# Softmax reciprocals as exp(-ln) on the activation engine, and one more pairwise add, in a fused attention and GeGLU block

## The chip, the cores and the metric

The kernel runs on one core of one Trainium2 chip. Its time is the device time of one launch in microseconds (us). The engines are named as in the profile: PE is TensorE (matmuls), PEld its weight loads, DVE is VectorE, ACT is ScalarE, POOL is GpSimd, and SP issues nearly all transfers.

## The reference

The input is 2048 tokens of width 512 in bf16. They are normalised once, and two branches read the result: a sliding, dilated local attention with 32 heads of width 16, where each token looks at itself and at the seven tokens 2, 4, ... 14 places back, and a gated feed-forward layer of hidden width 1376. The output is the input plus both branches.

```python
off = jnp.arange(8) * 2
idx = jnp.arange(S)[:, None] - off[None, :]
logits = jnp.einsum("bhsd,bhswd->bhsw", q, kg) * Dh ** -0.5
logits = jnp.where(idx >= 0, logits, -1e9)
attn = softmax(logits)                       # over the 8 places
o = jnp.einsum("bhsw,bhswd->bhsd", attn, vg)
...
h = gelu(g) * u                              # tanh form
return x + o @ wo + h @ w_down
```

## The kernel before, in words

The tokens are worked off in four blocks of 512 (b = 0 to 3 in all names). The weights stay in SBUF. Of a block, these steps matter here:

- Layer norm of 128-token tiles. For later tiles the sums and the scaling run on ACT (`bnst`, `bnag`, `sub`, `norm` and the small `ve`, `vp`, `va`, `vb`). A DMA transpose (`trx`) then puts the tile into `xnT`.
- Query, key and value products on PE (`mm`, L1009); ACT brings each 128x512 result out of PSUM (`evq`, `evk`, `evv`, L1020).
- Logits: DVE multiplies the queries with the eight shifted keys, one 128x4096 product for each of four head parts (`pr0` to `pr3` within a block, L1040), and adds the products in pairs (`pa_0`, `pa_1`, L1053). PE then sums over the head width with a matrix of ones, `er` (L1085), which accumulates the two pair sums into one pair of PSUM banks, 16 matmuls of 128x32 weights. Ahead of these, `er` also forms a part of the up projection (L1078).
- Softmax: DVE takes the maximum (`d1`, L1117) and subtracts it (`d2`, L1122); ACT takes the exponential into the tile EX (`exp`, L1131); DVE adds the eight exponentials in three steps (`d4a`, `d4b`, `d4c`, L1138) into the tile `ms`, takes the reciprocal in fp16 into `rc` (`d5`, L1150), and multiplies (`d6`, L1155) into the tile PB. SP stores PB to a scratch tensor in DRAM (`ss`, L1164) and loads it again, spread over the head width (`sl`, L1176), into the tile PT.
- Values: DVE multiplies by PT (`pv`, L1184) and adds (`pw`, `pz`), into the tile OT.
- Feed-forward: gate and up matmuls on PE (`fg`, `fu`, L1217), brought out of PSUM by ACT, the gate through gelu (`gelu`, L1227 and L1264), the up part by a plain copy (`uev`, L1234 and L1272). DVE multiplies them (`h`).
- Output: PE accumulates the feed-forward and attention parts (`acc`, L1302); ACT copies most results out (`fe`, L1335), DVE adds the input (`fin`), SP stores.

Each engine works off its own queue strictly in order. The orders are written out as five lists of task names, the table `ORDER`. A planner, `Graph.schedule`, takes these lists as they are; it walks them only to give buffers to tasks and to find which semaphore waits are needed. PSUM is one pool of eight banks, and a task that needs a bank waits for the readers of the one it is given. The pools for `ms`, PB and EX hold one buffer each.

Activations carry a label `table` ("sqrt", "exp", "gelu"), which only the planner's own costs use; loads of ACT's function tables are put into the program when it is built.

Of the kernel before, what the change touches and what calls it, by code (L numbers as in the profile page):

```python
# [135 lines left out]
class Graph:  # L136
# [252 lines left out]
    def report(self):  # L389
# [8 lines left out]
ACTF = mybir.ActivationFunctionType  # L398
# [6 lines left out]
    "pe":  # L405
        "warm0 warm1 warm2 warm3 warm4 warm5 warm6 warm7 warm8 warm9 tpx0_0 warm10 warm11 warm12 warm13 "
        "warm14 mma0_0 tpx0_1 mmt0_0 mmt0_1 mmt1_0 tpx1_0 mmt1_1 mmt0_2 tpx1_1 mmt1_2 mmt0_3 mmt1_3 "
        "mm0_2_0_0 mm0_2_3_0 mm0_2_2_0 mm0_2_1_0 fg0_0 fg0_1 fg0_2 fu0_0 fg0_3 fu0_1 fu0_2 fg0_4 fu0_3 fg0_5 "
        "fu0_4 fu0_5 fg0_6 fg0_7 er0_3 mm1_0_0_0 mm1_1_0_0 mm1_0_1_0 mm1_1_1_0 fg1_0 fu0_6 mm1_0_3_0 "
        "mm1_0_2_0 mm1_1_3_0 fu0_7 fu1_0 fg1_1 fg0_8 fu1_1 mm1_1_2_0 fu0_8 mm1_2_0_0 fg1_2 fg0_9 fu1_2 "  # L410
        "mm1_2_2_0 fg1_3 fu1_3 fu0_9 fg0_10 fg1_4 fu1_4 mm1_2_3_0 fg1_5 mm1_2_1_0 fg1_6 fu1_5 fu1_6 fg1_7 "
        "mm2_0_0_0 mm2_1_1_0 mm2_1_0_0 mm2_0_3_0 er1_3 mm2_0_1_0 fg1_10 mm2_1_2_0 mm2_2_1_0 mm2_0_2_0 fu1_7 "
        "fg2_0 accd1 mm2_1_3_0 accd2 fg2_1 mm2_2_3_0 mm2_2_2_0 fg1_8 fg2_2 acca0 fu2_0 accb0 fg1_9 mm2_2_0_0 "
        "accd3 er2_3 fu2_1 fu1_8 fu1_9 fu2_2 fg2_3 fu2_3 mm3_1_2_0 mm3_1_1_0 mm3_1_3_0 mm3_0_1_0 mm3_0_0_0 "
        "fg2_4 mm3_1_0_0 fu2_4 mm3_0_2_0 fg3_0 mm3_0_3_0 fu3_0 fg3_1 fg2_10 fg3_2 accd7 accd5 mm3_2_0_0 "
        "fg2_5 fu3_1 fg3_3 mm3_2_3_0 mm3_2_1_0 fu2_5 fu3_2 acca4 er3_3 accb4 fg3_4 accd6 fu3_3 fu3_4 fg2_6 "
        "fg3_5 fu2_6 fg2_7 fg3_6 fu2_7 fg2_8 fu2_8 fu3_5 fg3_7 fu3_6 mm3_2_2_0 fg2_9 fu3_7 fu2_9 fg3_8 fu3_8 "
        "fg3_9 fg3_10 acca8 accd10 accd9 fu3_9 accb8 accd11 acca12 accd13 accd14_0 accd14_1 accw14_0 "
        "accw14_1 accw13 accb12 accd15_0 accw12 accw15_0 accd15_1 accw15_1 accd15_2 accw15_2",
    "act":  # L420
        "c_tbl sx1 sq0 negm1 sxx1 sq1 evx0_0 evx0_1 evq0_0 sq2 evq0_1 evk0_0 evx1_0 sq3 evk0_1 bnst8 evx1_1 "
        "bnst9 evq0_2 sq6 evk0_2 evq0_3 evk0_3 ve8 evv0_0_0 sq4 vp8 bnag8 bnag9 va8 gelu0_0 evv0_2_0 "
        "evv0_3_0 bnst10 gelu0_1 bnst11 uev0_2 gelu0_3 vb8 gelu0_4 uev0_1 uev0_3 ve10 gelu0_5 uev0_4 uev0_0 "
        "uev0_5 gelu0_2 halo1 vp10 gelu0_7 bnag10 bnag11 evq1_0_0 evk1_0_0 evv0_1_0 evq1_1_0 evk1_1_0 "
        "gelu0_6 exp0 sub11 evq1_3_0 evk1_3_0 evq1_2_0 va10 uev0_7 uev1_0 uev0_10c uev0_6 sub9 vb10 sub8 "
        "uev1_1 evk1_2_0 norm9 uev0_10b gelu1_1 gelu1_0 norm8 gelu0_8 evv1_0_0 gelu1_2 sub10 uev0_8 bnst12 "
        "gelu0_9 norm11 uev1_2 uev0_9 norm10 evv1_2_0 gelu1_4 gelu1_3 uev1_3 evv1_1_0 uev1_4 uev1_5 uev0_10a "
        "bnst13 gelu1_5 gelu0_10 uev1_6 evk2_1_0 evv1_3_0 evk2_0_0 ve12 vp12 gelu1_7 bnag12 evq2_0_0 gelu1_6 "
        "evq2_1_0 uev1_10b bnag13 uev1_10c halv1 evk2_2_0 evq2_2_0 halo2 exp1 bnst14 sub12 bnst15 uev1_7 "
        "va12 ve14 vb12 uev1_10a vp14 bnag14 evk2_3_0 bnag15 evq2_3_0 evv2_1_0 va14 vb14 fe1 fe2 sub14 "  # L430
        "gelu2_0 evv2_2_0 halo3 gelu1_10 sub15 uev2_0 norm12 sub13 evv2_0_0 evv2_3_0 norm13 fe0 norm15 fe3 "
        "norm14 gelu1_8 gelu2_1 gelu1_9 uev2_1 uev1_8 uev2_2 uev1_9 uev2_3 gelu2_2 evk3_2_0 evk3_1_0 "
        "uev2_10b gelu2_3 exp2 evq3_1_0 evk3_3_0 evq3_2_0 evq3_0_0 halv2 evk3_0_0 uev2_10c evq3_3_0 uev2_4 "
        "uev2_10a gelu2_10 gelu3_1 uev3_0 gelu3_0 fe7 evv3_0_0 gelu2_5 gelu3_3 evv3_1_0 uev2_5 uev3_1 fe5 "
        "gelu2_4 gelu3_2 uev3_10c halv3 evv3_3_0 uev3_2 fe4 fe6 uev3_3 uev3_10b exp3 gelu3_5 uev2_6 gelu3_4 "
        "gelu2_7 uev2_7 uev2_8 gelu3_6 gelu2_6 evv3_2_0 gelu3_7 uev3_4 gelu2_8 gelu2_9 uev2_9 uev3_10a "
        "uev3_7 uev3_5 uev3_6 gelu3_10 fe10 gelu3_8 gelu3_9 uev3_9 fe9 uev3_8 fe8 fe11 fe13 fe12",
    "dve":
        "c_wdz bnst0 bnag0 sub0 rstd0 norm0 mean1 sub1 evy0_0 rstd1 norm1 evy0_1 bnst2 bnag2 sub2 rstd2 "
        "norm2 bnst3 bnag3 sub3 rstd3 norm3 bnst7 bnst6 bnst5 bnag6 bnag7 bnst4 bnag5 sub7 rstd6 bnag4 sub6 "  # L440
        "norm7 sub4 sub5 norm6 pr0_2 pr0_0 pr0_3 rstd4 pr0_1 norm4 norm5 pa0_1 pa0_0 h0_0 h0_1 h0_2 mask "
        "d1_0 d2_0 pr1_0 pr1_1 d4a_0 d4b_0 d4c_0 d5_0 rstd8 d6_0 pr1_3 pa1_0 pr1_2 h0_3 pa1_1 pv0_1 rstd10 "
        "pv0_3 h0_4 pv0_0 h1_1 pv0_2 pw0_1 h0_10 pw0_2 d1_1 pw0_3 d2_1 pz0 pr2_2 d4a_1 pr2_0 d4b_1 h1_3 "
        "d4c_1 h1_2 d5_1 h1_0 d6_1 pr2_1 pr2_3 pa2_0 fin1 rstd12 pa2_1 h1_10 pv1_1 rstd14 pv1_3 d1_2 pv1_0 "
        "d2_2 pv1_2 pw1_1 fin3 pw1_2 h2_1 pw1_3 h1_4 d4a_2 pz1 d4b_2 pr3_1 d4c_2 pr3_2 d5_2 fin0 d6_2 pr3_3 "
        "pr3_0 h2_0 h2_10 pa3_0 fin2 pa3_1 pv2_0 pv2_2 d1_3 pv2_1 d2_3 pw2_1 h3_1 d4a_3 h3_0 d4b_3 fin7 "
        "d4c_3 h2_2 d5_3 fin5 d6_3 pv2_3 pw2_2 h2_3 pw2_3 h2_4 pz2 fin4 pv3_3 pv3_0 pv3_1 fin6 pw3_1 fin10 "
        "h3_3 h3_10 pv3_2 h3_2 fin9 h3_4 pw3_2 fin8 pw3_3 fin11 pz3 fin14_0 fin14_1 fin13 fin15_0 fin15_1 "
        "fin12 fin15_2",
    "pool":  # L450
        "c_ones c_onef c_id c_vnpad c_idb c_eps c_mhalf c_e8a c_e8b c_e8c c_e8d c_ktpad c_mask0 c_mask1 "
        "c_utz sq8 sq10 sq12 sq14",
    "sp":
        "ld_x0_0 ld_x0_1 ld_wq ld_x1_0 ld_wk ld_x1_1 ld_wv ld_x2 ld_x4 ld_x3 ld_wg0 ld_wu0 ld_wt0 ld_x5 "
        "ld_wt1 trx3_0 ld_wt2 trx3_1 trx2_0 trx2_1 ld_wd0 ld_x6 ldxr1 ld_x7 ld_wd1 ld_wo ss0_2 ss0_3 ss0_0 "
        "ss0_1 ldxr2 sl0_1 sl0_3 sl0_2 trx4_0 sl0_0 trx4_1 trx5_1 trx5_0 ss1_2 ss1_3 ss1_1 ss1_0 sl1_1 sl1_3 "
        "sl1_0 sl1_2 ldxr3 trx6_0 trx6_1 trx7_1 trx7_0 sto3 sto1 ldxr0 ldxr7 ss2_1 ss2_2 ss2_3 ss2_0 sl2_0 "
        "sl2_3 sl2_2 sto0 sl2_1 sto2 ldxr5 ldxr4 sto5 ss3_0 ss3_1 ss3_2 ss3_3 ldxr10 sl3_3 sl3_0 sl3_2 sl3_1 "
        "ldxr6 sto4 sto6 ldxr8 ldxr9 sto9 ldxr11 ldxr14 sto8 sto7 sto10 ldxr13 sto11 sto14_0 sto14_1 ldxr15 "
        "ldxr12 sto13 sto15_0 sto15_1 sto12 sto15_2",  # L460
}
SCHED = dict(DMA_BPUS=290e3, DMA_FIXED=1.7)

# [5 lines left out]
def d_act(n):  # L469
    return 0.10 + 0.00085 * n  # L470
# [10 lines left out]
def bass_parallel_sum__sliding_local_dilated__glu_gated_geglu__prompt_kernel(nc, A_x, A_wqkv, A_wo, B_x, B_w_gate, B_w_up, B_w_down, out, dbg=None, cfg=None):  # L481
    cfg = dict(cfg or {})
# [26 lines left out]
    PACT = cfg.get("PACT", 4)  # L509
    PPOW = cfg.get("PPOW", 4)  # L510
    FIN2 = cfg.get("FIN2", tuple(range(14)))
    PR_ADD3 = cfg.get("PR_ADD3", ())
    WO_LAST = cfg.get("WO_LAST", (3,))
    CHAIN_SHIFT = cfg.get("CHAIN_SHIFT", [0, 300, 600, 900])
    FFN_BASE = cfg.get("FFN_BASE", 500)
# [8 lines left out]
    with contextlib.ExitStack() as es:  # L524
        block = es.enter_context(nc.Block())

        def sb(name, shape, dt):
# [14 lines left out]
        mask = sb("mask", [32, 2, 4, 16], F32)  # L542
        one_l = nc.const_aps.tensor(1.0, [128, 128], BF)
        one_r = nc.const_aps.tensor(1.0, [128, 512], BF)
        onef = sb("onef", [128, 2], F32)
# [4 lines left out]
        sums = sb("sums", [128, 3], F32)  # L550
# [6 lines left out]
        rc = sb("rc", [128, NMS, 128], FP16)  # L557
# [27 lines left out]
        G = Graph()  # L585
# [30 lines left out]
        I_onef = Item("onef")  # L616
# [25 lines left out]
            out=cf[:, :], in_=cf[:, :], pattern=[[-1, 128]], compare_op=ALU.is_equal, fill=0.0, base=0,  # L642
            channel_multiplier=1), rd=[I_cf], wr=[I_cf], prio=PC)
        G.task("pool", "c_idb", 0.65, lambda e: e.tensor_copy(out=ident[:, :], in_=cf[:, :]),
               rd=[I_cf], wr=[I_ident], prio=PC)
# [4 lines left out]
            out=E8f[:, :], in_=E8f[:, :], pattern=[[-4, 32]], compare_op=ALU.is_ge, fill=0.0, base=0,  # L650
            channel_multiplier=1), rd=[I_E8f], wr=[I_E8f], prio=PC2)
        G.task("pool", "c_e8c", 0.25, lambda e: e.affine_select(
            out=E8f[:, :], in_=E8f[:, :], pattern=[[4, 32]], compare_op=ALU.is_ge, fill=0.0, base=3,
            channel_multiplier=-1), rd=[I_E8f], wr=[I_E8f], prio=PC2)
        G.task("pool", "c_e8d", 0.25, lambda e: e.tensor_copy(out=E8[:, :], in_=E8f[:, :]),
               rd=[I_E8f], wr=[I_E8], prio=PC2)
        G.task("pool", "c_ktpad", 0.15, lambda e: e.memset(KT[:, KTI[0].slot, :, 0:16], 0.0), wr=[(KTI[0], "pad")],
               prio=PC2)
        G.task("pool", "c_vnpad", 0.15, lambda e: e.memset(VN[:, VNI[0].slot, :, 0:16], 0.0), wr=[(VNI[0], "pad")],
               prio=PC2)  # L660
# [4 lines left out]
            out=mask[:, :, :, :], in_=mask[:, :, :, :], pattern=[[8, 2], [2, 4], [1, 16]],  # L665
            compare_op=ALU.is_ge, fill=-1.0e9, base=-14, channel_multiplier=0),
            rd=[I_mask], wr=[I_mask], prio=PC2 + 10)
# [275 lines left out]
        for b in range(NB):  # L943
# [159 lines left out]
            def msv(k, it=it_ms):  # L1103
                return bass.AP(ms, (it.slot * 2 + k) * 128, [[NMS * 2 * 128, 128], [1, 128]])
# [22 lines left out]

            it_ex = Item("ex%d" % b, P_ex, "ex")

            def mk_d3(lgv=lgv):  # L1130
                return lambda e: e.activation(out=EX[:, :], in_=lgv(0, 128, [(1, 1024)]), func=ACTF.Exp)  # L1131
            G.task("act", "exp%d" % b, d_act(1024), mk_d3(), rd=[it_lg], wr=[it_ex], prio=base + 32,
                   table="exp", batch=b)

            for k, w in enumerate((512, 256, 128)):
                def mk_d4(w=w, it=it_pb, msv=msv):
                    def f(e):
# [6 lines left out]
                       rd=[it_ex if w == 512 else I_su], wr=[(it_ms, 1) if w == 128 else I_su],  # L1144
                       prio=base + 33)

            def mk_d5(msv=msv, it=it_ms):
                def f(e):
                    with nc.allow_low_precision(reason="the reference holds the sums of exponentials in bf16"):
                        return e.reciprocal(out=rc[:, it.slot, :], in_=msv(1))  # L1150
                return f
            G.task("dve", "d5_%d" % b, 0.87, mk_d5(), rd=[(it_ms, 1)], wr=[(it_ms, 2)], prio=base + 34)

            def mk_d6(it=it_ms, ito=it_pb):
                return lambda e: e.tensor_tensor(  # L1155
# [261 lines left out]
```

## Time and profile before

| | us |
|---|---|
| median of three runs | 184.02 (183.99 to 184.84) |
| the profiled execution | 184.58 |
| its span | 182.7 |
| PE busy | 178.9 |
| DVE busy | 169.6 |
| ACT busy | 128.4 |
| table loads on ACT, ten | 12.8 |

The span runs from the first to the last recorded instruction; some 1.8 us of the execution lie around it. Busy time is the union of an engine's instructions; ends of matmuls are modelled, so PE's busy time is not time at its peak. The granted clock was 1.00.

### The profile page before, as it was taken

The page shows a single profiled execution, that of the slowest core. Times are in us where ns is not written, and L with a number is a line of the kernel's source. Part 1 is how long each engine was busy: PE and PEld are TensorE (multiplying, and loading weights), DVE is VectorE, ACT ScalarE, POOL GpSimd, SP SyncE. Part 2 cuts the span into 40 slices and gives each one's busy share as a digit, 9 for nine tenths or more (in the row PEclk, how much of TensorE's full clock was granted, in tenths as well). Part 3 has the DMA queues.
Part 4 walks back from the last instruction along what each step waited for, and adds up shares of the span by engine and source line. Part 5 has one row for each costly group of instructions (what it writes and reads, how often), then busy time and mean ns, then how long its engine had stood idle before and what let it go on. Part 6 is the DMA issues. An engine that isn't in the chain of part 4 may idle for free.

```text
span 182.7 us, 2790 instructions
## 1 busy us (share of the span) xinstructions
PE 178.9 (98%) x1068; PEld 90.6 (50%) x1068; DVE 169.6 (93%) x172; ACT 128.4 (70%) x258; POOL 9.5 (5%) x23
## 2 busy tenths in 40 slices
PE   8999999999999999999999999999999999999994
PEld 2886444544444444444444544444444444444664
DVE  3769999999999999999999999999999999999922
ACT  5688987999999899998695977527449764234011
POOL 6000010003300000122000000000000000000000
PEclk9999999999999999999999999999999999999999
DMA  4999905932562000002851020128000346022433
GB/s 125 360 376 381 125 18 118 367 127 49 183 145 57 0 0 4 0 12 76 256 62 30 4 82 0 30 62 285 28 0 0 92 131 213 0 86 61 140 104 100
DMA packets 26221, 19.60 MB, mean 107 GB/s; under 512 B 13825, under 2 KB 23009, under 8 KB 26209
## 3 DMA queue, kind: packets, MB, share of 16 engines
q1 hardware_dynamic: 26208, 19.44, 37.0%
q8 instruction: 8, 0.13, 0.3%
q14 instruction: 5, 0.03, 0.1%
HBM read 14.71 MB, written 3.15 MB: 98 GB/s over the span
## 4 chain that ended last, share of the span: by engine, by line
PE 91%; DMA 4%; SPq 2%; ACT 1%; issue 0%; DVE 0%; DVEq 0%
PE PS L1217 38%; PE PS L1302 28%; PE PS L1009 19%; DMA XIN<-in_A_x_dram 4%; PE PS L1256 2%; PE PS L1085 2%; PE PS L1078 1%; PE PS L959 1%; SPq L731 1%; SPq L687 1%; ACT XS L769 0%; SPq L737 0%; ACT xnT L919 0%; DVE OB L1346 0%; DVEq L376 0%
## 5 line engine op out<-in xcount | busy, mean ns | idle before, releaser
L1302 PE MATMUL PS<-Wd,HT 128*128 128x512 bf16 (+2 forms) x209 | 41.0, 346 | 0.0
L1217 PE MATMUL PS<-xnT,Wg 128*128 128x512 bf16 x160 | 39.8, 379 | 0.0
L1217 PE MATMUL PS<-xnT,Wu 128*128 128x512 bf16 x160 | 39.1, 379 | 0.0
L1009 PE MATMUL PS<-xnT,Wqkv 128*128 128x512 bf16 x160 | 38.0, 380 | 0.0
L1184 DVE TENSOR_TENSOR UNI<-VN,PT 128x4096 f16<-128x4096 bf16 x16 | 36.3, 2287 | 0.0
L1040 DVE TENSOR_TENSOR UNI<-QT,KT 128x4096 f16<-128x4096 bf16 x16 | 36.1, 2286 | 0.0
L1302 PEld LDWEIGHTS PS<-Wd,HT 128*128 128x128 bf16 x209 | 19.6, 98 | 19.2 <-issue 0.4
L1234 ACT ACTIVATE UU<-PS 128x512 bf16<-128x512 f32 x40 | 23.1, 600 | 6.4 <-PE PS L1217 6.1
L1193 DVE TENSOR_TENSOR UNI<-UNI 128x4096 f16<-128x4096 f16 x12 | 27.5, 2290 | 0.0
L1227 ACT ACTIVATE GG<-PS 128x512 bf16<-128x512 f32 x40 | 22.9, 602 | 5.9 <-DVE HT L1241 5.8
L1009 PEld LDWEIGHTS PS<-xnT,Wqkv 128*128 128x128 bf16 x160 | 17.9, 113 | 16.9 <-issue 0.8
L1217 PEld LDWEIGHTS PS<-xnT,Wu 128*128 128x128 bf16 x160 | 15.6, 98 | 19.0 <-ACT XIN L853 0.4
L1217 PEld LDWEIGHTS PS<-xnT,Wg 128*128 128x128 bf16 x160 | 15.7, 98 | 18.7
L1335 ACT ACTIVATE OB<-PS 128x512 bf16<-128x512 f32 x14 | 8.3, 601 | 17.3 <-PE PS L1302 15.1
L1053 DVE TENSOR_TENSOR UNI<-UNI 128x4096 f16<-128x4096 f16 x8 | 18.2, 2286 | 0.0
L1302 PE MATMUL PS<-Wo,OT 128*128 128x512 bf16 (+2 forms) x76 | 16.5, 346 | 0.0
L1020 ACT ACTIVATE VN<-PS 128x512 bf16<-128x512 f32 x16 | 9.3, 597 | 6.5 <-PE PS L1009 6.5
L1241 DVE TENSOR_TENSOR HT<-GG,UU 128x1024 bf16<-128x1024 bf16 x20 | 13.6, 686 | 0.0
L832 POOL TENSOR_TENSOR sq<-ve,mhalf 128x2 bf16<-128x2 f32 x4 | 6.6, 1657 | 72.8 <-ACT ve L828 72.8
L1302 PEld LDWEIGHTS PS<-Wo,OT 128*128 128x128 bf16 x76 | 7.1, 98 | 6.6 <-issue 0.3
L1272 ACT ACTIVATE UT<-PS 64x256 bf16<-64x256 f32 (+1 forms) x12 | 5.4, 447 | 6.7 <-PE PS L1256 3.9
L959 PE MATMUL PS<-xnT,Wqkv 128*128 128x128 bf16 x128 | 8.3, 222 | 0.3 <-ACT xnT L919 0.2
(85 smaller groups left out, 159.5 us busy)
## 6 DMA issues: line engine op xcount, KB each, us to landing
PT<-pt_scratch SPq DMA_DIRECT2D x16, 256.0 KB, 4.2
XR<-in_A_x_dram SPq DMA_DIRECT2D x16, 128.0 KB, 2.2
out_dram<-OB SPq DMA_DIRECT2D x14, 128.0 KB, 1.9
Wqkv<-in_A_wqkv_dram SPq DMA_DIRECT2D x3, 512.0 KB, 5.0
XIN<-in_A_x_dram SPq DMA_DIRECT2D x6, 256.0 KB, 6.7
Wg<-in_B_w_gate_dram SPq DMA_DIRECT2D x1, 1280.0 KB, 8.6
Wu<-in_B_w_up_dram SPq DMA_DIRECT2D x1, 1280.0 KB, 11.6
Wd<-in_B_w_down_dram SPq DMA_DIRECT2D x1, 1280.0 KB, 6.6
```

What stands on the lines that cost most here:

```text
L959: ins = e.matmul(PS[:, 512 * it.slot + 128 * g:512 * it.slot + 128 * g + 128], lhsT=wcols(which, kt, g), rhs=xnT[:, itx.slot, kt, t * 128: ...
L1009: ins = e.matmul(PS[:, 512 * it.slot:512 * it.slot + 512], lhsT=wcols(which, kt, g), rhs=xnT[:, itx.slot, kt, :], start=(kt == 0), stop=(k ...
L1020: return e.activation(out=o, in_=PS[:, 512 * it.slot:512 * it.slot + 512], func=ACTF.Identity, scale=(QSC, 1.0, 1.0)[which])
L1040: return lambda e: e.tensor_tensor(out=UNI[:, it.slot, :, :], in0=bass.AP(QT, (itq.slot * 4 + g) * 512, [[NQT * 4 * 512, 128], [0, 8], [1, ...
L1053: return lambda e: e.tensor_tensor(out=UNI[:, i0.slot, :, :], in0=UNI[:, i0.slot, :, :], in1=UNI[:, i1.slot, :, :], op=ALU.add)
L1184: return lambda e: e.tensor_tensor(out=bass.AP(UNI, ito.slot * 4096, [[NUNI * 4096, 128], [2048, 2], [512, 4], [1, 512]]), in0=bass.AP(VN, ...
L1193: return lambda e: e.tensor_tensor(out=UNI[:, i0.slot, :, :], in0=UNI[:, i0.slot, :, :], in1=UNI[:, i1.slot, :, :], op=ALU.add)
L1217: ins = e.matmul(PS[0:M, 512 * it.slot:512 * it.slot + 512], lhsT=Wx[:, kt, j * 128:j * 128 + M], rhs=xnT[:, itx.slot, kt, :], start=(kt = ...
L1227: return lambda e: e.activation(out=GG[:, ito.slot, q, :], in_=PS[:, 512 * it.slot:512 * it.slot + 512], func=ACTF.Gelu_apprx_tanh)
L1234: return lambda e: e.activation(out=UU[:, ito.slot, q, :], in_=PS[:, 512 * it.slot:512 * it.slot + 512], func=ACTF.Identity)
L1241: return lambda e: e.tensor_tensor(out=HT[:, ito.slot, j - 1:j + 1, :], in0=GG[:, ig.slot, :, :], in1=UU[:, iu.slot, :, :], op=ALU.mult)
L1302: ins = e.matmul(PS[:, 512 * it.slot:512 * it.slot + CW], lhsT=(OT[:, ito.slot, q, ti * 128:(ti + 1) * 128] if kind == "o" else HT[:, ith. ...
```

## The change

In every block the reciprocal on DVE (`d5`) is replaced by two activations: `ln` takes the logarithm of the sums in place, and `d5`, now on ACT, takes the exponential of minus that into `rc`. A new activation `pre` takes the logarithm of a single constant into an unused place, and `exp` is ordered after it. All of them bear the table label "exp".

In the fourth block (b = 3) a third pairwise add on DVE, `pa3_2`, adds the two pair sums together, so that `er3` needs only one of them: 8 matmuls of L1085 instead of 16. The lists for PE, ACT, DVE and SP are written anew; POOL's list is the same.

```diff
-    PR_ADD3 = cfg.get("PR_ADD3", ())
+    PR_ADD3 = cfg.get("PR_ADD3", (3,))
...
+            t_pre = G.task("act", "pre%d" % b, 0.2, lambda e: e.activation(
+                out=onef[:, 1:2], in_=onef[:, 0:1], func=ACTF.Ln), rd=[(I_onef, 0)], wr=[(I_onef, 1)],
+                prio=base + 32, table="exp")
+
             def mk_d3(lgv=lgv):
                 return lambda e: e.activation(out=EX[:, :], in_=lgv(0, 128, [(1, 1024)]), func=ACTF.Exp)
...
+            G.order_after(t_ex, t_pre)
...
+            def mk_ln(msv=msv):
+                return lambda e: e.activation(out=msv(1), in_=msv(1), func=ACTF.Ln)
+            G.task("act", "ln%d" % b, 0.21, mk_ln(), rd=[(it_ms, 1)], wr=[(it_ms, 1)], prio=base + 34, table="exp")
+
             def mk_d5(msv=msv, it=it_ms):
-                def f(e):
-                    with nc.allow_low_precision(reason="the reference holds the sums of exponentials in bf16"):
-                        return e.reciprocal(out=rc[:, it.slot, :], in_=msv(1))
-                return f
-            G.task("dve", "d5_%d" % b, 0.87, mk_d5(), rd=[(it_ms, 1)], wr=[(it_ms, 2)], prio=base + 34)
+                return lambda e: e.activation(out=rc[:, it.slot, :], in_=msv(1), func=ACTF.Exp, scale=-1.0)
+            G.task("act", "d5_%d" % b, 0.21, mk_d5(), rd=[(it_ms, 1)], wr=[(it_ms, 2)], prio=base + 34, table="exp")
```

The lists around the softmax. ACT, block 0 and block 1:

```diff
-exp0 sub11 evq1_3_0 evk1_3_0 evq1_2_0 va10 uev0_7 uev1_0 ...
+pre0 exp0 sub8 bnag11 evk1_3_0 ln0 va10 uev0_5 evq1_3_0 d5_0 uev0_6 ...
-halo2 exp1 bnst14 sub12 bnst15 uev1_7 va12 ve14 vb12 ...
+bnst15 evv2_0_0 pre1 vb12 exp1 evq2_3_0 ve14 vp14 bnag14 ln1 bnag15 d5_1 va14 fe2 ... uev1_10b pre2 uev2_0 ...
```

ACT, blocks 2 and 3:

```diff
-gelu2_3 exp2 evq3_1_0 evk3_3_0 evq3_2_0 evq3_0_0 halv2 evk3_0_0 ...
+pre3 uev2_4 halo3 evv3_1_0 evq3_2_0 exp2 evk3_2_0 evq3_0_0 evk3_0_0 gelu2_5 evv3_0_0 evq3_1_0 evk3_1_0 uev3_0 ln2 evv3_3_0 d5_2 gelu2_10 ...
-uev3_10b exp3 gelu3_5 uev2_6 ...
+exp3 uev3_3 fe6 ln3 uev2_6 d5_3 gelu2_7 ...
```

DVE, blocks 0 to 3:

```diff
-h0_0 h0_1 h0_2 mask d1_0 d2_0 pr1_0 pr1_1 d4a_0 d4b_0 d4c_0 d5_0 rstd8 d6_0 ...
+h0_1 pr1_0 mask h0_0 d1_0 d2_0 pr1_1 d4a_0 d4b_0 d4c_0 pa1_0 d6_0 ...
-d2_1 pz0 pr2_2 d4a_1 pr2_0 d4b_1 h1_3 d4c_1 h1_2 d5_1 h1_0 d6_1 ...
+d2_1 pr2_2 d4a_1 d4b_1 d4c_1 pr2_1 d6_1 ...
-d4a_2 pz1 d4b_2 pr3_1 d4c_2 pr3_2 d5_2 fin0 d6_2 pr3_3 pr3_0 h2_0 h2_10 pa3_0 fin2 pa3_1 ...
+d4a_2 pr3_2 d4b_2 pz1 d4c_2 pr3_0 h2_1 d6_2 pr3_1 pa3_1 pa3_0 h2_10 fin0 pa3_2 ...
-d2_3 pw2_1 h3_1 d4a_3 h3_0 d4b_3 fin7 d4c_3 h2_2 d5_3 fin5 d6_3 ...
+d2_3 pv2_0 h2_2 d4a_3 pw2_1 d4b_3 fin3 d4c_3 pv2_2 h3_0 d6_3 ...
```

## The prediction

> **What bounds the kernel now.** I read the busy shares first, then the chain that ended last, then busy time by stretch, and last the timelines of ScalarE and VectorE around the softmax of one block.
>
> ```profile
> PE 178.9 (98%) x1068; PEld 90.6 (50%) x1068; DVE 169.6 (93%) x172; ACT 128.4 (70%) x258; POOL 9.5 (5%) x23
> ...
> PE 91%; DMA 4%; SPq 2%; ACT 1%; issue 0%; DVE 0%; DVEq 0%
> ```
>
> TensorE (PE) is the bound: from about 13 us on, the chain is one unbroken row of matmul groups, 0.86 us for four of 128x512. A microsecond that PE waits is a microsecond at the end. The averages hide a second fact, which the busy time by stretch shows (columns: stretch, length, then PE, PE weight load, DVE, ACT and POOL busy):
>
> ```profile
> 36.84:82.61 45.77, 45.77 (x238) 21.84 (x237) 45.52 (x38) 43.85 (x91) 5.22 (x3) 1.00 0.21 56
> 82.61:104.70 22.09, 22.09 (x129) 10.41 (x128) 21.83 (x17) 17.55 (x30) 0.70 (x1) 1.00 0.38 87
> 104.70:140.00 35.30, 35.30 (x190) 16.37 (x189) 35.28 (x29) 21.17 (x38) 0.00 (x0) 1.00 0.20 64
> ```
>
> From 36.84 us (the table load ahead of the first exp) to 82.61 us (the table load ahead of block 2's first gelu), PE and VectorE (DVE) have no slack and ScalarE (ACT) idles only 45.77 - 43.85 = 1.92 us. ACT's 70% is an average over this full stretch and a loose later part (4.5 us idle in the next 22, 14.1 us in the 35 after). Around the first softmax:
>
> ```profile
> 36.84 1.28 ACT L1131 ACT_TABLE_LOAD   x1
> 38.13 1.02 ACT L1131 ACTIVATE EX<-PS 128x1024 f16<-128x1024 f32 x1
> ...
> 40.48 0.95 DVE L1150 RECIPROCAL rc<-ms 128x128 f16<-128x128 f32 x1
> 41.35 0.11 DVE L803 RECIPROCAL rstd<-sq 128x2 f32<-128x2 bf16 x1
> 41.47 0.69 DVE L1155 TENSOR_TENSOR PB<-EX,rc 128x1024 bf16<-128x1024 f16 x1
> ```
>
> A table load takes 1.28 us of ACT, and the next instruction starts at its end. The reciprocal costs DVE 0.87 us (40.48 to 41.35), and the multiply that uses it follows without a wait.
>
> [...] The trace agrees on the load (x4 at exp, 1283 ns each)[...], so I use 1.283 us in all. [...] I read the built program's instruction order: there each Ln and each Exp that follows the other has a load ahead of it[...]. The shared set isn't used. [...] the trace agrees that it is dear: 950 ns for 128 elements, an add of that size 288 ns.
>
> **The change part by part.**
>
> *Table loads on ACT.* Before: 10 loads (one sqrt, four exp, five gelu). After, in the built order: 23. Block 0: Ln for `pre0`, Exp for `exp0`, Ln for `ln0`, Exp for `d5_0`, then gelu: three more than before. Block 1 the same, three more, and `pre2` comes soon after: a fourth. Gelus stand between the rest of blocks 2 and 3, where there are ten loads for four: six more. Together 13 x 1.283 = 16.7 us.
>
> *New activations.* `pre` on one element, four at 0.20 us (row L668, 203 ns) = 0.8 us. `ln` and `d5` on 128 elements are not in the trace[...]. Bounds: 0.2 us (an ACTIVATE of 2 elements) and 0.38 us (of 256).
>
> *Stretch 36.84 to 82.61.* The same content after the change holds 10 loads for 3, that is 7 x 1.283 = 9.0 us, three `pre` 0.6 us, two `ln` and two `d5` 1.2 us: 10.8 us more on an engine with 1.92 us to spare, so ACT is 8.8 us late at its end. The reordered queues don't shift this work out: the rest of that content is nearly the same. ACT empties PE's eight PSUM banks; PE can run ahead by at most eight groups, 8 x 0.865 = 6.9 us, and less in fact, because some banks hold logits and waiting gelus. What banks don't absorb, PE waits for.
>
> *VectorE.* It loses four reciprocals, 4 x 0.87 = 3.5 us, and gains `pa3_2`, which costs 2.20 us (one 128x4096 add start to start): 1.3 us less work. But it gains waits: `d6` needs `d5`, now behind other work and two loads on ACT. Let E be the end of `exp`. Steps are start-to-start times of the rows before.
> - Block 0: ACT runs `sub8` 0.61, `bnag11` 0.78, `evk1_3` 0.49, load and `ln0` 1.57, `va10` and two evictions 1.1, load and `d5_0` 1.57: ready at E + 6.1. DVE has three adds 1.1 and `pa1_0` 2.2: E + 3.3. Wait 2.8.
> - Block 0 again, ahead of E: `exp0` now stands behind two loads and `pre0`. With the Ln load at 36.8 as the Exp load was, E is 36.8 + 1.28 + 0.20 + 1.28 + 1.02 = 40.6. DVE ends `d2_0` near 36.7 (35.06 before, plus 2.2 for `pr1_0`, minus 0.6 for `h0_2`) and `pr1_1` at 38.9. Wait 1.7.
> - Block 1: ACT 1.6 of small work, 1.57, `bnag15` 0.78, 1.57: E + 5.5; DVE 1.1 + 2.2. Wait 2.2.
> - Block 2: ACT three evictions 1.45, gelu load and gelu 1.76, four evictions 1.9, 1.57, 0.48, 1.57: E + 8.7; DVE 6.9 of placed work. Wait 1.8.
> - Block 3: ACT E + 5.7, DVE E + 6.2. No wait; cover is `pv2_2` and `h3_0`, 2.8 us, and if it were gone the wait would be 2.3.
>
> Sum of waits 8.5, minus 1.3 of work: DVE +7.2 us. Its last big step before ends at 173.26 us (`pz3`) and PE's first reader starts at 173.74: nothing there absorbs it. Queued behind the waiting `d6` on DVE are the next block's products, which PE's `er` groups need, and the gated products and sums.
>
> *TensorE.* `er3` drops 8 of its 16 L1085 matmuls (0.86 us for 16): -0.43 us on the path. It waits now for `pa3_2`, at worst 2.2 us later; before, it started 1.4 us after its last sum. That is inside DVE's sum.
>
> *Queues.* SP's issues are reordered, none is added. The stores of `PB` follow `d6` and shift with it; from their issue (42.18) to the first `pv` (51.48) took 9.3 us, and the work now placed after `d6_0` is 8.5 us, after the others 9.5 or more: 0 to 0.8 us of new wait in block 0; I take 0. POOL's queue is the same.
>
> *Sum.* ACT says 8.8 less what banks absorb, DVE says 7.2 less some overlap or more through late evictions. These are two sides of one delay, not addends. I take +7.9, less PE's 0.43: +7.5 us. On the profiled execution (span 182.7, 184.58 in all) that is 192.1; the median, 184.02, lies 0.56 below that execution, so 191.5.
>
> **The rivals.**
> 1. *Banks and cover absorb most (0.13).* Half of the DVE waits vanish because ACT runs closer to its inputs: 4.2 - 1.3 = +2.9: 187. For it: before, PE never waited although ACT was 96% busy. Against it: 8.8 us is more than eight banks.
> 2. *ACT's lag all lands on PE and block 2 adds its own (0.10).* 8.8 + 1.8 for `d6_2` + 2.2 for `pa3_2`: +12.8, near 197[...]. Against it: ACT's 18.7 us of idle between 82.61 and 140.
> 3. *Not slower (0.07).* The lag at the end of block 1 stays under the 6.9 us of banks and DVE keeps its 1.3 us: PE then gains its 0.43 us, 183.6. It decides at one place: `er1` and `er2` must not find their product sums late. A closer packing of the new order could add the 0.4 us of gaps PE has left, and perhaps a shorter start: under 183.1. Against it: 1.92 us of idle for 10.8 us of work.
> 4. *The change doesn't do what it says*: the second half of it (one set for ln and exp) indeed does not hold in the built order. That is my main case.
>
> **How the numbers follow.** Main case 0.70, 191.5, own range 188.5 to 195. About 0.5% (0.9 us) is what a measurement of this kernel can tell from no change, so cases 1, 2 and main are slower: 0.93. Rival 3 gives 0.04 within 0.5% and 0.03 faster. Range: 187 (rival 1's value) to 196.5 (just short of rival 2's).
>
> **What would show it.** In the profile after: 23 table loads, 29.5 us; no L1150 reciprocals; ACT near 148 us busy; DVE idle on ACT ahead of the multiply into PB, some 2 us in each of blocks 0 to 2, none in block 3; PE idle on ACT between 45 and 95 us, 6 to 8 us; L1085 with 56 matmuls; the span near 190. I am wrong if the loads number 12, if loads overlap with activations, or if PE shows no idle in that stretch.

## The result and the profile after

The changed kernel takes 191.92 us (191.82 to 192.19), 1.042 times the kernel before (95% interval 1.0389 to 1.045). Its profiled execution took 192.02 us with a span of 190.3, 7.6 longer than before. The forecast was 191.5, range 187 to 196.5.

Busy time and, below it, the shares of the chain that ended last, from the page of the changed kernel:

```profile
PE 178.0 (94%) x1043; PEld 88.9 (47%) x1060; DVE 169.0 (89%) x169; ACT 146.1 (77%) x283; POOL 9.2 (5%) x23
...
PE 43%; DVE 26%; ACT 20%; DMA 7%; issue 1%; SPq 1%; DVEq 0%
```

PE has lost no work to speak of, but 12 us of its span are idle where it was 4. The chain, which was 91% PE, now passes through ACT and DVE for 46% of the span. The same three stretches as before (PE, PE weight load, DVE, ACT, POOL busy):

```profile
36.84:82.61 45.77, 43.36 (x222) 19.95 (x225) 42.03 (x33) 44.74 (x91) 2.93 (x2) 1.00 0.22 54
82.61:104.70 22.09, 19.87 (x91) 8.91 (x91) 19.31 (x15) 20.62 (x38) 2.15 (x1) 1.00 0.37 81
104.70:140.00 35.30, 34.29 (x200) 16.10 (x203) 33.45 (x28) 28.36 (x47) 0.00 (x0) 1.00 0.20 60
```

PE loses 2.4, 2.2 and 1.0 us in them, DVE 3.7, 2.8 and 1.9. Who waits for whom is in DVE's waits (us in total, times, longest):

```profile
DVE PB L1161 <- ACT rc L1157: 6.4, 3, 2.8
...
DVE HT L1285 <- ACT GG L1270: 1.2, 1, 1.2
...
DVE SU L1143 <- ACT EX L1135: 0.6, 1, 0.6
```

PE's own waits, beside its start, are nearly all for ACT, 6.8 us in all: for banks or results that an eviction, a gelu or `exp` has still to finish.

```profile
PE PS L1223 <- ACT GG L1233: 2.0, 1, 2.0
PE PS L1223 <- ACT UU L1240: 1.9, 2, 1.2
PE PS L1308 <- ACT OB L1341: 1.5, 1, 1.5
PE PS L1009 <- ACT EX L1135: 0.7, 2, 0.5
PE PS L1009 <- ACT GG L1233: 0.7, 1, 0.7
```

On DVE the multiply into PB (`d6`, now L1161) waits three times for the new exponential. ACT's timeline in block 0 shows what stands ahead of it, DVE's what that does:

```profile
36.80 1.28 ACT L1135 ACT_TABLE_LOAD   x1
38.09 1.02 ACT L1135 ACTIVATE EX<-PS 128x1024 f16<-128x1024 f32 x1
...
40.93 1.28 ACT L1153 ACT_TABLE_LOAD   x1
42.23 0.31 ACT L1153 ACTIVATE ms<-ms 128x128 f32<-128x128 f32 x1
...
43.62 1.28 ACT L1157 ACT_TABLE_LOAD   x1
44.91 0.31 ACT L1157 ACTIVATE rc<-ms 128x128 f16<-128x128 f32 x1
...
40.15 2.28 DVE L1053 TENSOR_TENSOR UNI<-UNI 128x4096 f16<-128x4096 f16 x1
45.25 0.69 DVE L1161 TENSOR_TENSOR PB<-EX,rc 128x1024 bf16<-128x1024 f16 x1 [2.83 <-ACT rc L1157]
```

Between `exp` and `d5` ACT switches its table twice, for two activations of 0.31 us. DVE has one add as cover (`pa1_0`, done at 42.4) and then stands still for 2.83 us, with the next products behind it in its queue.

### The profile page after: what moved, and what is told of

The parts are those of the page before. It is cut to its first block, busy times and chain, and to the rows that moved or that the text cites. A ratio compares the mean times of both kernels' runs of the same rounds, so it can differ in the third digit from the quotient of the medians.

```text
span 190.3 us, 2774 instructions
## 1 busy us (share of the span) xinstructions
PE 178.0 (94%) x1043; PEld 88.9 (47%) x1060; DVE 169.0 (89%) x169; ACT 146.1 (77%) x283; POOL 9.2 (5%) x23
## 4 chain that ended last, share of the span: by engine, by line
PE 43%; DVE 26%; ACT 20%; DMA 7%; issue 1%; SPq 1%; DVEq 0%
PE PS L1223 19%; PE PS L1308 14%; PE PS L1009 8%; DVE UNI L1190 7%; DVE UNI L1199 5%; DVE UNI L1040 5%; DMA Wg<-in_B_w_gate_dram 5%; DVE UNI L1053 3%; ACT L1157 3%; DMA Wqkv<-in_A_wqkv_dram 3%; ACT L1130 2%; ACT L1153 1%; ACT L1135 1%; ACT UU L1240 1%; DVE PS L1122 1%
## 5 line engine op out<-in xcount | busy, mean ns | idle before, releaser
L1223 PE MATMUL PS<-xnT,Wg 128*128 128x512 bf16 x158 | 38.4, 379 | 3.5 <-ACT GG L1233 2.0
L1308 PE MATMUL PS<-Wd,HT 128*128 128x512 bf16 (+2 forms) x205 | 40.5, 345 | 0.3
L1009 PE MATMUL PS<-xnT,Wqkv 128*128 128x512 bf16 x156 | 37.2, 380 | 1.8 <-ACT EX L1135 0.7
L1199 DVE TENSOR_TENSOR UNI<-UNI 128x4096 f16<-128x4096 f16 x12 | 27.4, 2280 | 0.0
L1053 DVE TENSOR_TENSOR UNI<-UNI 128x4096 f16<-128x4096 f16 x9 | 20.4, 2283 | 0.0
L1161 DVE TENSOR_TENSOR PB<-EX,rc 128x1024 bf16<-128x1024 f16 x4 | 2.8, 688 | 6.4 <-ACT rc L1157 6.4
```

Of the source, the lines that this page charges most:

```text
L1009: ins = e.matmul(PS[:, 512 * it.slot:512 * it.slot + 512], lhsT=wcols(which, kt, g), rhs=xnT[:, itx.slot, kt, :], start=(kt == 0), stop=(k ...
L1053: return lambda e: e.tensor_tensor(out=UNI[:, i0.slot, :, :], in0=UNI[:, i0.slot, :, :], in1=UNI[:, i1.slot, :, :], op=ALU.add)
L1199: return lambda e: e.tensor_tensor(out=UNI[:, i0.slot, :, :], in0=UNI[:, i0.slot, :, :], in1=UNI[:, i1.slot, :, :], op=ALU.add)
L1223: ins = e.matmul(PS[0:M, 512 * it.slot:512 * it.slot + 512], lhsT=Wx[:, kt, j * 128:j * 128 + M], rhs=xnT[:, itx.slot, kt, :], start=(kt = ...
L1308: ins = e.matmul(PS[:, 512 * it.slot:512 * it.slot + CW], lhsT=(OT[:, ito.slot, q, ti * 128:(ti + 1) * 128] if kind == "o" else HT[:, ith. ...
```

## The experiments

My theory was that the switches of table are the cause: 23 loads where the program needs 12. The rivals were the way over ACT as such (a result that waits behind other work), the newly written orders, and the added add. A second question was how the loads cost: by ACT's total time or by DVE's wait ahead of `d6`. Each ratio is to the kernel before on the same chip, whose median there was 184.3 to 184.4; differences between runs are differences of their medians. A needless load is one of a set that is already there.

**One shared set.** Only the choice of set changes: a load of one set that serves both `ln` and `exp` is put in by hand ahead of `pre0`, `pre1`, `pre3`, `ln2` and `exp3` (in the edit it stands at the first dots). The trace then has 12 loads, these five, six for gelus and one at the start; no other load stands ahead of a `pre`, `exp`, `ln` or `d5`.

```diff
+            def shared(name, f):
+                def g(e):
+                    if name in SHARED:
...
+                    return f(e)
+                return g
...
-"exp%d" % b, d_act(1024), mk_d3(),
+"exp%d" % b, d_act(1024), shared("exp%d" % b, mk_d3()),
...
+SHARED = ('pre0', 'pre1', 'pre3', 'ln2', 'exp3')
```

> Same queues, same activations and the same add as the changed kernel; only the table set is chosen by hand, one that serves both ln and exp, so ACT has 12 loads in place of 23 (11 x 1.283 = 14.1 us less on ACT). If the loads are the cause (my theory): the 7.9 us come back but for at most 1 us, so 183.6 to 185, and DVE's waits for rc shrink from 6.4 us to under 1 us. If the way over ACT is the cause (the result waits behind other ACT work, loads or not): still 188 or more, with over 3 us of waits for rc. If the new orders or the added DVE add are the cause: no change, 191 to 192.

Measured: 183.94 us, ratio 0.9976 (0.9966 to 0.9986). All 7.9 us came back, and the kernel is a little faster than before. DVE's wait for `rc`, and the first stretch, in this kernel:

```profile
DVE PB L1170 <- ACT rc L1166: 0.5, 1, 0.5
```

```profile
36.84:82.61 45.77, 45.77 (x239) 21.67 (x237) 45.63 (x36) 41.94 (x94) 7.41 (x3) 1.00 0.21 59
```

The way over ACT, the new orders and the added add are all still there; none of them costs the 7.9 us. PE is unbroken again, and ACT idles 3.8 us in this stretch, twice what it did before the change.

**The same set, 23 loads again, behind the waits.** `SHARED` now names every `pre`, `exp`, `ln` and `d5`.

> The shared set as in the run before, but with a load of it ahead of every pre, exp, ln and d5, so that the loads number 23 again, at the same places as in the changed kernel; nothing else differs. If a load costs its 1.28 us whatever set it brings: 191.9, within 0.5. If the switch between different sets[...] has a cost of its own: clearly under 191.9, near 184 to 188.

Measured: 196.43 us, ratio 1.0652 (1.0621 to 1.0684), 4.5 us over the changed kernel; I had expected 191.9 or less. The trace shows a difference that I had overlooked: these loads stand behind the semaphore wait of their activation, where those of the changed kernel stand ahead of it (its `ln3` loads at 144.15 us and only then waits 0.58 us, last section). In block 3 of this run:

```profile
141.43 1.28 ACT L1134 ACT_TABLE_LOAD   x1 [1.24 <-DVE PS L1123]
...
147.50 1.28 ACT L1134 ACT_TABLE_LOAD   x1 [1.88 <-DVE ms L1152]
```

ACT waits 1.24 and 1.88 us and only then loads. DVE's waits for `rc` are 8.1 us, four of them, where they were 6.4 and three. Behind these loads PE stands still for 2.5 us, and its clock falls for some microseconds (last section).

**23 loads, ahead of the waits.** The same loads, emitted ahead of the waits (at the second dots).

```diff
         for t in self.order[eng_name]:
...
+            if eng_name == "act" and t.name in SHARED:
...
             for (s, v) in t.waits:
                 e.wait_ge(s, v)
```

> As in the run with one set and 23 loads, but each load is placed ahead of its activation's semaphore wait, as the loads of the changed kernel are, and not behind it. If a load costs the same whatever set it brings, and the 4.5 us by which the former run was slower than the changed kernel came from loads that could no longer run during the wait: 191.9, within 0.7. If hand-placed loads are dearer in themselves: 195 or more. If it was the switch between different sets: under 190.

Measured: 191.9 us, ratio 1.0423 (1.0406 to 1.044): the changed kernel's time. A load costs the same although it brings a set that is already there, and with the loads put back the whole loss is back. Eleven needless loads cost 8.0 us, 0.73 each.

**Where they cost: blocks 0 and 1 alone.** `SHARED` is the list of 12 loads and `exp0 ln0 d5_0 exp1 ln1 d5_1`.

> One shared set; the six loads that are not needed are put in around the softmax of blocks 0 and 1 alone (18 loads), the rest as with 12 loads (183.9). By my prediction the tight stretch before 82 us is where most is lost: of the 8 us, 5 to 6.5: 189 to 190.5. If the lag of blocks 0 and 1 were made good later (ACT is loose after 85 us): 184 to 186.

Measured: 188.11 us, ratio 1.0211 (1.0195 to 1.0228), 4.2 us over one set: below my 5 to 6.5. DVE's waits for `rc` are 4.6 us, but they are not on the chain that ended last, which runs over PE and ACT. PE waits 3.6 us for ACT, above all for evictions that stand behind the loads:

```profile
PE 82%; ACT 14%; DMA 1%; issue 1%; SPq 0%; DVE 0%; DVEq 0%
...
PE PS L1227 <- ACT UU L1244: 1.9, 2, 1.2
PE PS L1312 <- ACT OB L1345: 1.5, 1, 1.5
...
PE PS L1013 <- ACT EX L1139: 0.2, 1, 0.2
```

**Blocks 2 and 3 alone.** `SHARED` is the 12 and `pre2 exp2 d5_2 ln3 d5_3`.

> The counterpart: five needless loads in blocks 2 and 3 (pre2 among them, which runs right after block 1's softmax), 17 loads. By my prediction 1.8 us of waiting in front of d6 in block 2 and the one load in the tight stretch: 1.5 to 3 us over 183.9, so 185.4 to 187. If loads count alike wherever they stand, 5/11 of 8 us: 187.5. If the later part has room for all: 184.

Measured: 187.17 us, ratio 1.0165 (1.0148 to 1.0182), 3.2 us over one set: above my 1.5 to 3. Two waits on DVE make up most of it (with one set they are 0.5 and 0.4 us):

```profile
DVE PB L1165 <- ACT rc L1161: 1.8, 1, 1.8
DVE HT L1289 <- ACT GG L1274: 1.6, 1, 1.6
```

The second is a gelu (`gelu1_10`) that is late behind the load for `pre2`. The two runs add up to 7.4 of the 8.0 us, at 0.70 and 0.65 us per needless load: ACT's loose later part makes such a load hardly cheaper.

**Loads behind `d5` in blocks 0 and 1.** The six needless loads of the run with 18 are written directly behind `d5_0` and `d5_1` instead, three each (the edit against that run):

```diff
-SHARED = ('pre0', 'exp0', 'ln0', 'd5_0', 'pre1', 'exp1', 'ln1', 'd5_1', 'pre3', 'ln2', 'exp3')
+SHARED = ('pre0', 'pre1', 'pre3', 'ln2', 'exp3', 'uev0_6', 'uev0_6', 'uev0_6', 'va14', 'va14', 'va14')
...
-            if eng_name == "act" and t.name in SHARED:
+            for _ in range(SHARED.count(t.name) if eng_name == "act" else 0):
```

> One shared set and the six needless loads of blocks 0 and 1, as in the run with 18 loads (188.1), but all three of a block directly behind d5, where nothing of the softmax waits for them. ACT's work is the same. If ACT's total work in the stretch is what costs (1.283 x 6 = 7.7 us against about 3.8 us that ACT idles there with one set): near 188 again. If it is DVE's wait in front of d6 (4.6 us in that run, for loads between exp and d5): 184 to 185.5. My prediction took the two as one delay, so I expect something between, 186.

Measured: 184.44 us, ratio 1.0008 (0.9995 to 1.0021), 0.5 us over one set. But the run is not what its expectation says. Of three loads written one behind the other the trace has one:

```profile
40.98 0.31 ACT L1161 ACTIVATE rc<-ms 128x128 f16<-128x128 f32 x1
41.30 1.28 ACT L376 ACT_TABLE_LOAD   x1
42.60 0.60 ACT L1244 ACTIVATE UU<-PS 128x512 bf16<-128x512 f32 x1
...
L376 ACT ACT_TABLE_LOAD x7 | 9.0, 1283 | 0.1
```

Seven loads put in by hand, with seven of the build's, make 14: two are needless, not six. ACT is busy for 134.6 us, where the run with 18 loads has 139.6. Two loads, 2.6 us, fit into the 3.8 us that ACT idles in the first stretch with one set. So nearly no loss is what both answers forecast, ACT's total time and DVE's wait ahead of `d6`, and the run does not decide between them. It shows that a load right behind `d5` cost under 0.3 us, where those around `exp`, `ln` and `d5` cost 0.70.

**Loads behind `d5` in every block** (and one at `pre2`, as in the changed kernel): `pre2 gelu2_10 gelu2_10 gelu2_7 gelu2_7` added to the list.

> The same for all blocks: 23 loads as in the changed kernel, the needless ones of every block behind its d5 (one at pre2 as before). If ACT's total work costs: 191 to 192. If the waits in front of d6 do: 184 to 186. Between: 188.

Measured: 186.3 us, ratio 1.0101 (1.008 to 1.0121), 0.3 above the range for DVE's wait. Here too one load of each row is left: 17 in all, not 23, five of them needless, so the difference from the changed kernel is one of number as well as of place. The fair comparison is with the run that has its five needless loads in blocks 2 and 3: 17 loads there too, ACT busy for 138.5 us and here for 138.3, but 187.17 us there, 0.9 more, and the intervals of the two ratios lie apart. So place counts at an equal number of loads, though two of the five here also stand in other blocks. No wait for `rc` is listed any more. Of the 1.9 us over the run before, a wait for `gelu1_10` behind the load at `pre2` is the largest part (1.8 us, there 0.5).

**Which way the delay takes: open.** The start of `d6` in the four blocks (us, from the timelines) shows where DVE falls behind. The queues are the same in all three kernels:

| | block 0 | 1 | 2 | 3 |
|---|---|---|---|---|
| one set, 12 loads | 41.65 | 78.73 | 117.38 | 141.40 |
| changed kernel, 23 | 45.25 | 84.17 | 124.93 | 148.71 |
| blocks 0 and 1 alone, 18 | 44.89 | 83.80 | 121.45 | 145.47 |

The changed kernel is 3.6 us late after the first softmax, 5.4 after the second and 7.6 after the third, and makes almost nothing of it good. But PE, waiting for evictions, falls behind in the same places, and in the run with 18 loads DVE wins back 1.0 of its 5.1 us while the end stays at the 4.2 us by which PE is late. That the loads cost the time is shown; whether DVE's wait ahead of `d6` alone would cost as much as the late evictions do, no run here tells. It would take loads that delay the one and not the other.

**The changed kernel without `pre`**, sets chosen by the build (the task and its place in the order are taken out).

> The changed kernel without the four one-element logarithms, its sets chosen by the build as before; each costs a switch of its own there, so 19 loads for 23 and 0.8 us less of pre: 5.9 us less on ACT. At the 0.65 to 0.7 us per load that the runs with 17 and 18 loads showed: 2.6 to 3.4 us less than 191.9, so 188.5 to 189.3. If loads ahead of exp are covered (0.6 us of waiting for EX in the changed kernel's profile): 190.5 to 191.5.

Measured: 188.61 us, ratio 1.0224 (1.0208 to 1.0239), in the range I gave. The one-element logarithms, which only bring a set, cost 3.3 us. Waits for `rc` are 4.6 us in place of 6.4, and the waits for `gelu1_10` and EX are gone.

**The new orders with the reciprocal on DVE**, just ahead of `d6`; no `pre` or `ln`.

```diff
-act: ... pre0 exp0 sub8 bnag11 evk1_3_0 ln0 va10 uev0_5 evq1_3_0 d5_0 ...
+act: ... exp0 sub8 bnag11 evk1_3_0 va10 uev0_5 evq1_3_0 ...
-dve: ... d4c_0 pa1_0 d6_0 ...
+dve: ... d4c_0 pa1_0 d5_0 d6_0 ...
```

> The new orders and the added add, with the reciprocal on DVE just ahead of d6 again and no pre, ln or d5 on ACT; 10 loads. If the loads are the cause: 183.5 to 185.5 (DVE has 3.5 us more work than with one set, but no waits for rc; PE's 8 matmuls stay saved). If the new orders are the cause: 188 or more.

Measured: 186.28 us, ratio 1.0101 (1.0065 to 1.0138), 0.8 over my range. These orders need the time on DVE that the reciprocal leaves: with it back they are 2.3 us slower than with one set. So the idea of the change is worth that much in these orders where the loads are right; against the kernel before, which has the reciprocal on DVE in other orders, it is 0.25%.

**The added add alone**, in the old orders: `PR_ADD3` is `(3,)`, with `pa3_2` behind `pa3_1`.

> The kernel before with the added add alone, right behind the second pair sum, and er3 cut to 8 matmuls. By the sum of my prediction: DVE has no slack, so 2.2 us more of it against 0.43 us less of PE: 185 to 186.2. If PE alone sets the end and DVE's 2.2 us find cover: 183.6 (0.43 less). If the added add were behind a large part of the loss: 188 or more.

Measured: 186.73 us, ratio 1.013 (1.0098 to 1.0161), 2.4 over before and 0.5 over my range. The interval, 1.8 to 3.0 us, holds the add's 2.2 us in full; what my sum gave, 2.2 less PE's 0.43, lies just below it. Either way DVE had no slack for the add in the old orders.

**One set without the added add**: `PR_ADD3` is `()`, `pa3_2` taken out, 12 loads ahead of the waits.

> One shared set, 12 loads, the new orders, but without the added add of block 3; er3 has 16 matmuls again. PE has 0.43 us more and DVE 2.2 us less. If PE alone sets the end with one set: 184.3 (183.9 + 0.4). If DVE still sets part of it: 182.5 to 183.7, which would be the fastest version.

Measured: 184.86 us, ratio 1.0024 (1.0012 to 1.0035), 0.9 slower than one set with it; I expected at most 0.4. So in the new orders, with DVE relieved, the add pays. DVE's 2.2 us less bring nothing: it waits as long for the logits of block 3 (with one set 0.2 us):

```profile
DVE ms L1121 <- PE PS L1089: 2.2, 1, 2.2
```

PE's 8 matmuls explain 0.43 of the loss; where the rest goes I did not find out. It is hardly the place of the 12 loads, ahead of the waits here and behind them in the run with one set: the next run has them ahead too.

**One set without `pre`**, 12 loads ahead of the waits.

> One shared set, 12 loads ahead of the waits, and the four one-element activations left out, whose only use was to bring the set: 0.8 us less on ACT. PE sets the end and waits little: 183.5 to 184, at best 0.3 under the run with one set (183.9). If ACT still limits somewhere: up to 1 us under it, 183.0.

Measured: 183.83 us, ratio 0.9975 (0.9961 to 0.999): no different from one set with `pre`. These two are the fastest versions, 0.25% under the kernel before. PE is busy throughout all three stretches in both, so there is little left for the softmax to give.

## Why the prediction was right, and where its steps were not

- **The build doesn't take the shared set: right.** 23 loads of 1283 ns, with 0.01 to 0.02 us to the next instruction. That one set can serve both functions the run with one set shows (12 loads, 183.94 us); it took a load placed by hand to get it, and that was worth the whole 7.9 us. ACT is busy for 146.1 us; I had said near 148.
- **DVE's waits: right in place and nearly in size.** Forecast for `d6` in blocks 0 to 3: 2.8, 2.2, 1.8 and none; measured 2.83, 1.76, 1.85 and none. The wait for EX in block 0 was 0.59, not 1.7: ACT began the load for `pre0` at 35.28, and I had put it at 36.8, the place of the old load; that term was mis-sized by 1.1 us. A term was missing: `gelu1_10` late behind the load for `pre2`, 1.2 us. And DVE's busy time fell by 0.6 us, where I had counted 1.3 us less work. The steps of 1.57 us take 0.29 us for a `ln` or `d5`: an estimate of mine, between the bounds of 0.20 and 0.38; measured 0.31. The errors nearly cancel: 8.5 us of waits forecast, 8.2 measured; less work 1.3 and 0.6; so 7.2 forecast, and 7.6 measured, the growth of the span.
- **ACT's total time: too large.** I counted 8.8 us of lag at 82.6 us, by more work against 1.92 us of idle. The step that failed is "The reordered queues don't shift this work out". With one set ACT idles 3.8 us in that stretch, where the old idle time less the new activations (1.8: three `pre` of 0.20 us, four `ln` and `d5` of 0.31) would have left 0.1. A load for `pre0` just ahead of the stretch (35.15 us) explains 1.3 of them; the other 2.4, an estimate from these numbers, are room that the new orders made. The lag that the trace shows is smaller: the changed kernel starts `d5` of block 1 at 83.83 us, the one with one set at 77.56, 6.3 us earlier. "Two sides of one delay" still stands: both show up, and the runs don't separate them.
- **The sum: near in part by luck.** The 7.9 us that I took before PE's 0.43 lay between the two sums, and one of them was too large; DVE's alone would have given 184.02 + 7.2 - 0.43 = 190.8.
- **Where PE loses: right in cause and total, wrong in place.** I said 6 to 8 us of idle on ACT between 45 and 95 us. PE's waits for ACT are 6.8 us in all, but between 45 and 95 us it idles only 2.5 (50.00 less 47.46, in the line below). It loses 4.6 us from 36.84 to 104.7 us, 1.0 up to 140 and 2.0 in one wait for a gelu at 150 us.
- **PE's 0.43 us: right in count** (56 matmuls of L1085), hidden under the rest in the changed kernel.
- **Rivals.** Rival 1 would have halved the waits ahead of `d6`; they came in full. Rival 2's 12.8 us did not come: ACT's lag was smaller than its first term. Rival 3 named a small gain if the loads did no harm, 183.6; the run with one set shows 183.94.

The changed kernel from 45 to 95 us (columns as above):

```profile
45.00:95.00 50.00, 47.46 (x242) 22.18 (x247) 46.71 (x39) 48.84 (x100) 5.08 (x3) 1.00 0.29 76
```

## What to carry to other kernels

Where functions alternate on the activation engine, count the table loads in the trace before you trust that they share a set: a set that serves both helps only if it is the one loaded (here 12 loads and 183.94 us, else 23 and 191.92). Don't price a load by its time alone. Around `exp`, `ln` and `d5`, where PE's evictions and DVE's multiply wait behind it, a needless load of 1.28 us cost some 0.7; right behind `d5`, with idle time left on ACT, under 0.3; and the same 23 loads cost 4.5 us more behind their semaphore waits than ahead of them. When two engines are late at once, move the suspected work past one wait and keep its amount. Then count in the trace whether the amount was kept: six loads that I wrote were two there, and the run that was to decide between two answers could not.

## What the runs showed of the hardware

Three things I had not expected. A table load placed ahead of a semaphore wait runs during the wait, and 23 loads there cost 191.9 us where 23 behind it cost 196.4. In block 3 of the changed kernel ACT loads first and then still waits for DVE's sums:

```profile
144.15 1.28 ACT L1153 ACT_TABLE_LOAD   x1
146.01 0.31 ACT L1153 ACTIVATE ms<-ms 128x128 f32<-128x128 f32 x1 [0.58 <-DVE ms L1143]
```

A load of the set that is already there takes its 1283 ns as any other where an activation stands between the two (1.28 us at 41.30 us in the run with loads behind `d5` in blocks 0 and 1, 1283 ns the mean of its seven); of several written one behind the other the trace has only one (eleven written there, seven in the trace). And the granted clock of PE fell for one stretch after a stall, in the run with the 23 loads behind the waits (columns as above, the granted clock after POOL):

```profile
150.00:154.00 4.00, 1.51 (x7) 0.47 (x5) 3.04 (x3) 3.96 (x7) 0.00 (x0) 0.93 0.08 20
154.00:158.00 4.00, 4.00 (x13) 1.54 (x12) 4.00 (x5) 2.05 (x5) 0.00 (x0) 0.64 0.21 49
158.00:162.00 4.00, 4.00 (x21) 1.77 (x19) 3.13 (x4) 2.06 (x4) 0.00 (x0) 1.00 0.73 218
```

PE, busy for 1.51 us of four, comes back at 0.64 of its clock for about four microseconds and does 13 matmuls where it does 20 or 21: some 1.5 us lost beside the stall (an estimate: 7 matmuls of 0.216, a quarter of the 0.865 of a group of four). The longest wait in it was 2.5 us. A wait of 2.3 us in the same run brought no second fall of that size: the mean clock of the run is 0.990, and the two low rows explain nearly all of that (0.07 and 0.36 of four microseconds, 1.7 of 194.8). The longest wait of the changed kernel, 2.0 us, left its mean at 1.000. One case gives no threshold.
